# Transposing q and k of the first three units in bf16 to contiguous PSUM columns, with a refitted plan

## The chip, the core and the metric

The kernel runs on one core of a Trainium2 chip. The core's engines work side by side, each through its own queue in order: TensorE (PE in the profile; its weight loads are shown apart as PEld), VectorE (DVE), ScalarE (ACT), GpSimd (POOL) and SyncE (SP), which here mostly issues transfers (DMA). A wait at the head of a queue holds all that stands behind it. The metric is the device time of one execution in microseconds (us). For the kernel before it is 219.11 us, the median of three runs (218.81 to 219.12).

## What is computed

Attention with a local window and a few global keys, followed by a feed-forward block with softplus. The reference, cut to what matters:

```python
# q, k, v: (4, 8, 768, 64), n_global = 8, n_local = 96
scores = np.matmul(q, k.transpose(0, 1, 3, 2)) / np.sqrt(64)
rel = pos[:, None] - pos[None, :]
is_global = pos[None, :] < n_global
is_local = (rel >= 0) & (rel < n_local)
dist = np.where(is_global & ~is_local, n_local, np.abs(rel))
scores = scores - slopes[:, None, None] * dist
a = softmax(np.where(is_global | is_local, scores, -1e9))
x = np.matmul(a, v)                     # then (4 * 768, 8 * 64)
h = x @ w_in                            # w_in: (512, 2048)
g = np.maximum(h, 0.0) + np.log1p(np.exp(-np.abs(h)))
out = g @ w_out                         # w_out: (2048, 512), out: (3072, 512) float32
```

## The kernel before, in words

The 3072 tokens are 24 blocks of 128; two blocks of one batch entry make a unit, and there are 12 units (`UNITS`), numbered in the order in which they are worked on. A unit passes these stages:

- `load_unit` brings q, k and v by DMA into slots `raw`. q and k of the first three units (`WIDE`) come in two halves each, v and everything later in one piece. `load_w` brings slabs of w_in and w_out (`i0` to `i7` and `o0` to `o7`), half a megabyte each. `FIRST_LOADS` lists the first loads, the planner decides their order.
- `cast_q` (L841) and `cast_rows` (L865) convert them to bf16 (`qb`, `kb`, `vb`), on the engine that the table `CHOICE` names. Slabs are converted at L823.
- The transposes bring the head dimension to the partitions (`qT`, `kT`, `kTa`). Units 0 to 2 do this on PE (`transp_pe`, L926), later units by a DMA transpose (`transp_dma`, L953). In `transp_pe` eight matmuls against the identity write f32 to two banks of the scores' PSUM tiles `s_ps`. They write with a step, so that the columns stand in PSUM in the order of `qT`, four apart, and the copy out of PSUM (L936 for one bank of 512 columns, L939 for both banks in one instruction) reads contiguously.
- `scores` (L1058, L1005 for block 0) multiplies, DVE adds the bias into `z` (L1084; blocks 0 and 1 get theirs from PE, L995 and L1039), ACT takes exponentials (L1018, L1091), PE multiplies by v (L1110), DVE divides by the sum (L1121, L1122), PE (L1141) or a DMA transposes the result into `XT`, for the PE ones with a copy at L1146. `globals_k` (L966) and `globals_v` (L976) copy the global keys and values into the block before.
- Two blocks make a group. `mm1` (L1168) multiplies by w_in in eight steps of eight matmuls into two banks `h_ps`; each step is followed by an exponential (L1183), each pair of steps by a logarithm (L1194), which together are the softplus `g`. `mm2` (L1217) multiplies by w_out into `o_ps` (`s_ps` for group 0), `store` copies (L1246) and writes the result (L1249).

The order is not the order of the code. Every piece is an operation of a `Planner`, with an engine, an expected duration and a rank. `due` works ranks back from wanted times and adds a correction of each operation from the table `NUDGE`; `run` then plays the queues and writes the instructions in the order in which they start. Its constants (`FETCH`, `DMA_FIRST` and so on) and its durations shape only that order. Thirty-five dummy matmuls (`filler`, L1330, called `fill0` to `fill34`) have the lowest rank of all: PE gets one whenever nothing else was ready in the plan, until they are used up. The waits in the program follow from what each instruction reads and writes; tiles in PSUM are guarded bank by bank.

Of the kernel before, what the change touches and what calls it, by code (L numbers as in the profile page):

```python
# [23 lines left out]
class Planner:  # L24
# [5 lines left out]
    FETCH = 15.5  # L30
    FETCH_COST = 1.0
    DMA_FIRST = 0.75
# [181 lines left out]
PE_KEYS = {  # L214
# [3 lines left out]
}  # L218
# [47 lines left out]
    "a0.0": -2,  # L266
    "a0.1": -14.5,
    "a0.2": -3,
    "a0.4": 2.25,
    "a1.0": -1,  # L270
    "a1.1": -4.25,
    "a1.2": -3.5,
    "a1.3": -0.5,
    "a1.4": 0.5,
    "a1.6": 15,
    "a1.7": -2,
    "a2.0": 8,
    "a2.2": -11,
    "a2.3": 1.5,
    "a2.4": 4,  # L280
    "a2.5": -10.25,
    "a2.6": -4,
    "a2.7": 8,
    "b0.0.2": 10.5,
    "b0.0.4": -8.5,
    "b0.0.8": -8,
    "b0.1.0": 0.5,
    "b0.1.10": -7.5,
    "b0.1.12": -14.75,
    "b0.1.14": 2.75,  # L290
    "b0.1.2": -1,
    "b0.1.4": 3.75,
    "b0.1.6": -40.75,
    "b0.1.8": 2.75,
    "b1.0.0": 4.75,
    "b1.0.10": 4.5,
    "b1.0.12": -11,
    "b1.0.14": -2,
    "b1.0.2": 1,
    "b1.0.4": -0.5,  # L300
    "b1.0.8": -18.25,
    "b1.1.0": 4.25,
    "b1.1.10": -0.5,
    "b1.1.12": 0.25,
    "b1.1.4": 0.5,
    "b1.1.6": 10,
    "b1.1.8": 55.75,
    "biasFalse0": 2.25,
    "biasFalse2": -2,
    "biasFalse4": 5.5,  # L310
    "biasFalse5": -6.75,
    "biasFalse6": 10,
    "biasFalse7": -5.25,
    "biasTrue0": 1.75,
    "biasTrue2": -2,
    "biasTrue3": 2,
    "biasTrue4": -4,
    "biasTrue6": -0.5,
    "biasTrue7": -1.5,
    "blank": -7,  # L320
    "castk0.0": -2.25,
    "castk0.1": -11.25,
    "castk1.1": 11.5,
    "castk2.0": 4,
    "castk2.1": -8.25,
    "castk3.00": 4.5,
    "castk3.01": -2.5,
    "castk3.10": -0.25,
    "castk3.11": 1,
    "castk4.00": 3.5,  # L330
    "castk4.11": -0.25,
    "castq0.1": 23.25,
    "castq1.1": 16,
    "castq2.0": -17.25,
    "castq2.1": 1.5,
    "castq3.0": 7,
    "castq5.0": 9,
    "castv0.01": 3.5,
    "castv0.10": -1.25,
    "castv0.11": 3,  # L340
    "castv1.00": -13.5,
    "castv1.01": 4,
    "castv1.10": 4,
    "castv1.11": -4.5,
    "castv2.00": 6.5,
    "castv2.01": 8,
    "castv2.10": 8.5,
    "castv2.11": 1.25,
    "castv3.00": 0.75,
    "castv3.10": 0.25,  # L350
    "castv3.11": -20,
    "castv4.00": 1,
    "castv4.10": 0.25,
    "castv4.11": -8,
    "castv6.10": -0.5,
    "castv6.11": -8,
    "cin1": -10,
    "cin2": -3.25,
    "cin3": -67.25,
    "cin4": -0.5,  # L360
    "cin5": -6,
    "cin6": -0.25,
    "cin7": 29,
    "cout0": -6.75,
    "cout1": -19.5,
    "cout3": 0.75,
    "cout4": 2.5,
    "cout6": 6,
    "cout7": -3.25,
    "cpk0.0": -2.75,  # L370
    "cpk1.0": 20.25,
    "cpk1.1": 6.75,
    "cpk2.0": -2,
    "cpk2.1": 9,
    "cpq0.0": 7.25,
    "cpq1.0": -1.25,
    "cpq2.0": 3,
    "d0": -4.25,
    "dl0a": -0.25,
    "dl0b": -0.25,  # L380
    "dl0c": -0.25,
    "dl1a": 0.5,
    "dl1e": 2.5,
    "e0.1": 3.75,
    "e0.2": -4,
    "e0.3": -18.75,
    "e0.4": -1,
    "e0.6": -0.5,
    "e1.0": -2,
    "e1.1": 2,  # L390
    "e1.2": -23,
    "e1.3": 12.5,
    "e1.5": 0.5,
    "e1.6": -1,
    "e1.7": -9.75,
    "e2.3": 2.75,
    "e2.4": -0.5,
    "e2.5": 11.25,
    "ex0.0": 0.75,
    "ex0.1": -8,  # L400
    "ex2.0": -67.75,
    "ex2.1": 2.25,
    "ex3.0": 6.5,
    "ex3.1": -1.5,
    "ex4.0": -23.5,
    "ex4.1": 3.75,
    "ex5.0": -0.25,
    "ex5.1": -26,
    "ex6.0": 0.5,
    "ex6.1": 8.5,  # L410
    "ex7.0": 23.75,
    "ex7.1": 3.75,
    "gk4": 0.5,
    "gk6": 11.75,
    "gk8": 12,
    "gv4.0": -0.75,
    "gv4.1": 1.25,
    "gv5.0": -1,
    "gv5.1": 12,
    "gv6.0": 7,  # L420
    "gv6.1": -6,
    "gv7.1": 0.25,
    "gv8.0": -8,
    "gv8.1": 1,
    "ident": 9.75,
    "iota": -1,
    "ldk0.0": -2,
    "ldk0.1": -6.25,
    "ldk1.0": -5.25,
    "ldk2.0": 0.25,  # L430
    "ldk2.1": 26,
    "ldk3": -4,
    "ldk4": 10.5,
    "ldk5": 1.75,
    "ldq0.0": 1,
    "ldq0.1": 23,
    "ldq1.1": -4,
    "ldq2.0": 12.5,
    "ldq2.1": -4.25,
    "ldq3": -4,  # L440
    "ldv0": 13,
    "ldv3": -8.75,
    "ldv4": -9.5,
    "ldv5": 4,
    "ldv6": -2,
    "ldv7": 16.75,
    "ldv8": 8,
    "ln0.0": 16.5,
    "ln0.2": 4.75,
    "ln0.3": -8.5,  # L450
    "ln1.0": -15,
    "ln1.2": 2,
    "ln2.0": -177.75,
    "ln2.1": 8.75,
    "ln2.2": -8,
    "nm1.0": -12,
    "nm2.0": 7.25,
    "nm2.1": 1,
    "nm3.0": -1,
    "nm3.1": -1,  # L460
    "nm5.0": 2,
    "nm6.0": -12,
    "nm6.1": 1,
    "oc0.0.0": 4,
    "oc0.1.0": 30.25,
    "oc1.0.0": -8,
    "pv0.0": 12,
    "pv0.1": -17.75,
    "pv1.0": -4,
    "pv1.1": 1.25,  # L470
    "pv2.0": 12,
    "pv2.1": -13.75,
    "pv3.0": 0.25,
    "pv3.1": 5.5,
    "pv4.1": 1,
    "pv5.0": -4,
    "pv5.1": 1,
    "pv6.0": 3,
    "pv6.1": -3.25,
    "sb0.0": 2.25,  # L480
    "sb1.1": 17.5,
    "sc0.0": -8,
    "sc1.0": 8,
    "sc1.1": 7.75,
    "sc2.0": 0.5,
    "sc3.0": 9,
    "sc4.0": 7.25,
    "sc5.1": 2,
    "sc6.0": 0.5,
    "sc7.0": -2.25,  # L490
    "st0.0.0": 7.25,
    "st0.1.0": -0.25,
    "st1.0.0": 1,
    "table": -3,
    "trk0.0": 1.5,
    "trk1.0": 1.5,
    "trk1.1": 72.5,
    "trk2.0": -24.5,
    "trk2.1": 1.5,
    "trk4": -2.5,  # L500
    "trq0.0": -36.5,
    "trq1.0": 2,
    "trq2.0": 4,
    "trq2.1": 0.5,
    "trq3": 0.25,
    "trq5": 0.25,
    "win1": -0.5,
    "win5": -16,
    "win6": 1,
    "wout0": -12.5,  # L510
    "wout1": -1.75,
    "wout2": -18.5,
    "wout4": 3.75,
    "wout5": 2,
    "wout7": -11.75,
    "xc1": 5.25,
    "xc2": 1,
    "xc3": 1.75,
    "xc4": 0.25,
    "xc5": -6.5,  # L520
    "xt1": 2,
    "xt2": -82.5,
    "xt4": 5.25,
    "xt5": -2,
    "xt6": -6.75,
    "z2.0": 0.25,
    "z3.0": -8.25,
    "z4.0": -2,
    "z4.1": 15,
    "z5.0": -2,  # L530
    "z6.0": 8,
    "z6.1": -47.25,
# [22 lines left out]
    "biasFalse0": "POOL",  # L555
    "biasFalse2": "DVE",
    "biasFalse5": "DVE",
    "biasTrue0": "DVE",
    "biasTrue1": "DVE",
    "biasTrue2": "DVE",  # L560
    "biasTrue3": "POOL",
# [5 lines left out]
    "castk2.0": "POOL",  # L567
    "castk3.00": "ACT",
    "castk3.01": "ACT",
    "castk3.10": "DVE",  # L570
    "castk3.11": "ACT",
    "castk4.00": "DVE",
    "castk4.01": "ACT",
    "castq0.0": "POOL",
# [3 lines left out]
    "castq4.0": "POOL",  # L578
    "castq5.0": "POOL",
    "castv0.00": "DVE",  # L580
    "castv0.01": "POOL",
    "castv0.10": "ACT",
    "castv1.00": "DVE",
    "castv1.01": "POOL",
    "castv1.10": "DVE",
    "castv2.11": "ACT",
    "castv3.00": "ACT",
    "castv3.01": "DVE",
    "castv3.10": "ACT",
    "castv3.11": "DVE",  # L590
    "castv4.01": "ACT",
    "castv4.10": "ACT",
    "castv4.11": "ACT",
    "cin1": "ACT",
    "cin3": "DVE",
    "cin5": "DVE",
    "cin6": "DVE",
    "cout3": "ACT",
    "cout6": "DVE",
    "cout7": "DVE",  # L600
    "cpk0.0": "DVE",
    "cpk1.1": "ACT",
    "cpk2.1": "DVE",
    "cpq0.0": "ACT",
    "cpq2.1": "ACT",
    "gk4": "ACT",
    "gk5": "ACT",
    "gk6": "ACT",
    "gk7": "ACT",
    "gv4.0": "ACT",  # L610
    "gv4.1": "ACT",
    "gv5.0": "ACT",
    "gv6.0": "DVE",
    "gv8.0": "DVE",
    "oc0.0.0": "ACT",
    "xc1": "ACT",
    "xc4": "ACT",
# [13 lines left out]
def kernel(  # L631
# [116 lines left out]
    def held(keys):  # L748

        return sorted({key[:2] for key in keys})  # L750
# [13 lines left out]
    def load_unit(i, rank, only="qkv"):  # L764
# [4 lines left out]
        for z, which in enumerate(only):  # L769
# [25 lines left out]
            op(f"ld{which}{i}", "SP", 0.45, rank + 0.01 * z, fn, dma=(2.5 if (which, i) == ("v", 0) else 1.8, 30.0), sync=sync,  # L795
# [95 lines left out]

    def kt_unit(i):
        name, slot = kt_tile(i)
        return {"kTa": kTa, "kT": kT}[name][slot][:]
# [16 lines left out]
    def v_keys(n):  # L911
        return [("vb", vb_slot(n), r) for r in range(2)]

    def transp_pe(i, which, banks, engs, rank):


        src = {"q": qb, "k": kb}[which][i % NQB][:].rearrange("p a h d -> p (a h d)")
        dst = qT[i % NQT][:] if which == "q" else kt_unit(i).rearrange("p x m t -> p (x m) t")
        for rs in ((0, 1),) if len(held(banks)) == 1 else ((0,), (1,)):

            def mm(rs=rs):
                for r in rs:
                    tr = bank(banks[r]).rearrange("p (x m g a) -> p a x g m", x=2, m=NPAIR, a=4)
                    for a in range(4):
                        c = P * (2 * a + r)
                        nc.tensor.matmul(tr[:, a], src[:, c : c + P], ident[:])  # L926
# [573 lines left out]
```

## Time and profile before

| what | us |
|---|---|
| median of the runs | 219.11 |
| the profiled execution's own time | 219.03 |
| its span in the trace | 217.2 |
| PE busy | 211.7 |
| ACT busy | 170.7 |
| DVE busy | 115.7 |
| POOL busy | 74.4 |
| transposes of q and k on PE: from 6.79 to 33 us, 48 matmuls | 5 of the chain of waits |

The page gives, for each engine, busy time and share of the span, and then the span in 40 slices of 5.43 us, each with a digit for the busy share (9 is 90% or more). The chain of waits is followed back from the last instruction: at each step to whatever released it. The timeline lists instructions in order of start: start in us, duration, engine, line, operation, tile written `<-` tiles read, shape, count; in square brackets stands the engine's idle time before it and who ended it. The duration of a matmul includes the time to pass through the array, and consecutive matmuls overlap, so their pace is read from start to start. The granted TensorE clock is full in every slice.

### The profile page before, as it was taken

How to read it: one execution, taken by the hardware profiler on the slowest of the kernel's cores; microseconds unless marked ns; L12 is line 12 of the kernel's file. 1: busy time of each engine (PE TensorE's matmuls, PEld its weight loads, DVE VectorE, ACT ScalarE, POOL GpSimd, SP SyncE). 2: the span in 40 equal slices, each digit the busy share in tenths (PEclk: the TensorE clock that was granted, in tenths of full speed). 3: DMA queues.
4: the chain of work that ended last, by engine and by line, in shares of the span. 5: the costliest groups of instructions: out<-in, count | busy, mean ns of one | idle time of the engine just before them, and what ended most of it. 6: DMA issues, size and time to landing. Idle time of an engine off the chain costs nothing.

```text
span 217.2 us, 4970 instructions
## 1 busy us (share of the span) xinstructions
PE 211.7 (97%) x2003; PEld 144.5 (67%) x2003; DVE 115.7 (53%) x216; ACT 170.7 (79%) x236; POOL 74.4 (34%) x127
## 2 busy tenths in 40 slices
PE   7899999999999999999999999999999999999994
PEld 2576887656665787757767767756766767767554
DVE  6568868674489667327546546446545952101121
ACT  4899999999995699978788688678697878788300
POOL 6316333253059525900265274233236320000000
PEclk9999999999999999999999999999999999999999
DMA  5999999999999399945895996892687212011112
GB/s 202 333 367 387 386 357 367 317 286 214 225 317 175 104 236 264 211 108 155 147 231 160 159 218 165 207 165 72 127 209 198 69 30 75 0 48 53 48 48 97
DMA packets 69846, 40.95 MB, mean 188 GB/s; under 512 B 30144, under 2 KB 61248, under 8 KB 69824
## 3 DMA queue, kind: packets, MB, share of 16 engines
q1 hardware_dynamic: 69392, 40.05, 72.1%
q10 hardware_dynamic: 432, 0.59, 0.9%
q8 instruction: 15, 0.25, 0.5%
q14 instruction: 7, 0.06, 0.1%
HBM read 27.26 MB, written 6.29 MB: 154 GB/s over the span
## 4 chain that ended last, share of the span: by engine, by line
PE 83%; ACT 12%; DMA 2%; issue 2%; SPq 0%; DVE 0%
PE h_ps L1168 34%; PE o_ps L1217 30%; PE s_ps L1058 5%; PE x_ps L1110 4%; ACT pb L1091 3%; ACT e L1183 3%; PE s_ps L1217 3%; PE s_ps L926 2%; DMA raw<-in_k_dram 2%; PE x_ps L1217 2%; ACT g L1194 2%; PE x_ps L1330 1%; ACT vb L976 1%; ACT XT L1146 1%; ACT kb L865 1%
## 5 line engine op out<-in xcount | busy, mean ns | idle before, releaser
L1168 PE MATMUL h_ps<-XT,w_in_bf 128*128 128x256 bf16 x768 | 95.8, 273 | 0.9 <-ACT e L1183 0.7
L1168 PEld LDWEIGHTS <-w_in_bf 128*128 128x128 bf16 x768 | 73.6, 98 | 18.7 <-issue 1.7
L1217 PE MATMUL o_ps<-w_out_bf,g 128*128 128x512 bf16 (+1 forms) x320 | 77.7, 371 | 0.0
L1183 ACT ACTIVATE e<-h_ps 128x512 f32<-128x512 f32 x96 | 59.5, 627 | 20.9 <-PE h_ps L1168 20.5
L1217 PEld LDWEIGHTS <-g 128*128 128x128 bf16 x416 | 37.3, 98 | 28.6
L1084 DVE TENSOR_TENSOR z<-s_ps,biasA 128x1024 f32<-128x1024 f32 x38 | 45.8, 1219 | 15.2 <-PE s_ps L1058 8.6
L1194 ACT ACTIVATE g<-e 128x1024 bf16<-128x1024 f32 x48 | 50.7, 1057 | 1.3
L1091 ACT ACTIVATE pb<-z 128x1024 bf16<-128x1024 f32 (+1 forms) x44 | 43.1, 988 | 7.9 <-DVE z L1084 7.9
L1246 DVE COPY osb<-o_ps 128x512 f32<-128x512 f32 (+1 forms) x20 | 13.4, 670 | 37.1 <-PE o_ps L1217 37.1
L976 POOL COPY vb<-vb 4x512 bf16<-4x512 bf16 x27 | 16.4, 608 | 33.0 <-PE x_ps L1110 28.6
L865 POOL CAST vb<-raw 64x512 bf16<-64x512 f32 x33 | 20.4, 617 | 18.0 <-DMA raw<-in_v_dram 16.8
L865 POOL CAST kb<-raw 64x512 bf16<-64x512 f32 x30 | 18.6, 619 | 19.5 <-DMA raw<-in_k_dram 18.4
L1110 PEld LDWEIGHTS <-pb 128*128 128x128 bf16 x352 | 16.5, 98 | 6.1 <-ACT pb L1091 0.2
L1122 DVE TENSOR_TENSOR xs<-x_ps,rcp 128x256 bf16<-128x256 f32 x40 | 17.0, 424 | 1.4
L1121 DVE RECIPROCAL rcp<-x_ps 128x4 f32<-128x4 f32 x40 | 7.2, 179 | 18.7 <-PE x_ps L1110 18.3
L1110 PE MATMUL x_ps<-vb,pb 128*128 128x65 bf16 x304 | 15.9, 193 | 0.0
L1217 PE MATMUL s_ps<-w_out_bf,g 128*128 128x512 bf16 (+1 forms) x64 | 13.6, 352 | 0.0
L1330 PE MATMUL x_ps<-blank 128*128 128x512 bf16 x35 | 11.1, 442 | 1.2 <-DVE blank L1269 1.2
L1058 PEld LDWEIGHTS <-kT 64*128 64x128 bf16 x224 | 6.8, 94 | 5.1 <-issue 4.9
L1058 PE MATMUL s_ps<-qT,kT 64*128 64x128 bf16 x224 | 9.9, 218 | 0.0
L1084 DVE TENSOR_TENSOR z<-s_ps,bias 128x512 f32<-128x512 f32 x6 | 3.9, 687 | 7.3 <-PE s_ps L1058 7.3
L1246 ACT COPY osb<-x_ps 128x128 f32<-128x128 f32 x1 | 0.3, 266 | 8.7 <-PE x_ps L1217 8.7
(84 smaller groups left out, 120.7 us busy)
## 6 DMA issues: line engine op xcount, KB each, us to landing
raw<-in_v_dram SPq DMA_DIRECT2D x12, 512.0 KB, 5.7
out_dram<-osb SPq DMA_DIRECT2D x23, 256.0 KB, 2.3
raw<-in_q_dram SPq DMA_DIRECT2D x9, 512.0 KB, 4.5
raw<-in_k_dram SPq DMA_DIRECT2D x9, 512.0 KB, 5.6
raw<-in_moe_w_in_dram SPq DMA_DIRECT2D x8, 512.0 KB, 9.5
raw<-in_moe_w_out_dram SPq DMA_DIRECT2D x8, 512.0 KB, 8.6
raw<-in_k_dram SPq DMA_DIRECT2D x6, 256.0 KB, 6.0
raw<-in_q_dram SPq DMA_DIRECT2D x4, 256.0 KB, 8.0
```

Source lines behind the costliest of these rows:

```text
L865: copy_on[eng](dst, src)
L976: copy_on[eng](vb_of(prev)[sl, :, 0:D], vb_of(first)[sl, :, 0:D])
L1058: nc.tensor.matmul(reg if unit_of(n) in WIDE else reg.rearrange("p (r t) -> p r t", r=2), kt[rows, 2 * part + m, :], qv(rows, 2 * part + m ...
L1084: nc.vector.tensor_tensor(z, src, bias, ALU.add)
L1091: nc.scalar.activation(pb[:, 0:nr, :].rearrange("p (y a) b -> p y (a b)", y=2), src, AF.Exp, scale=1.0 / root_d)
L1110: nc.tensor.matmul(xv[:, h, :], pb[:, 4 * (h % 2) + 2 * part + h // 2 if lone else u_all * (2 * (h % 2) + h // 2) + u, :], vb_of(prev if u ...
L1122: nc.vector.tensor_tensor(xs[:, 4 * part : 4 * part + 4, :], xv[:, :, 0:D], rcp[:][:, :, None].to_broadcast([P, 4, D]), ALU.mult,)
L1168: last = nc.tensor.matmul(hv[:, j, :], w_in_bf[:, m, fb * P : fb * P + P], XT[g % NXG][:, m, :], start=(m == 0), stop=(m == NM - 1),)
L1183: nc.scalar.activation(e[:, p % 2, :, :].rearrange("p j (b t r) -> p (j b) r t", b=2, r=2), hb[:].rearrange("p (a r t) -> p a r t", a=4, r=2),
L1194: nc.scalar.activation(gt[:, 2 * p - 2 : 2 * p + 2, :].rearrange("p a t -> p (a t)"), e[:].rearrange("p a j t -> p (a j t)"), AF.Ln, bias=1.0,
L1217: nc.tensor.matmul(bank(key)[:, 0 : z - a], gt[:, fb, ns * P : ns * P + P], w_out_bf[:, fb, a:z], start=(fb == 0), stop=(fb == NFB - 1),)
L1246: copy_on[eng](osb[:, a:z], bank(key)[:, 0 : z - a])
```

## The change

Four things change, of which the last reorders the whole program:

- In `transp_pe` the eight transposes of one matrix write bf16 into one PSUM bank, each to 128 contiguous columns, rather than f32 with a step into two banks. The step moves into the copies: each half (512 columns) is read with four nested steps, the innermost over `a`, 128 columns apart, and written contiguously.
- There are always two copies of 512 for one matrix, each on an engine of its own by `CHOICE` (DVE or ACT); both read the same bank. Before, units 0 and 1 had three copies of 1024 and two of 512, unit 2 had four of 512.
- `globals_k` spells its access with one dimension more, for the same elements.
- The planner's constants, the tables `NUDGE` (every correction) and `CHOICE` (casts, biases and copies put on other engines) are fitted anew. So the order on every queue differs, that of the first loads on SP too. `FIRST_LOADS`, the sizes of the loads and the number of dummies stay.

```diff
-    FETCH = 15.5
+    FETCH = 18.0
-    DMA_FIRST = 0.75
+    DMA_FIRST = 0.62
...
 PE_KEYS = {
-    0: (("s", 1, 0), ("s", 1, 1), ("s", 0, 0), ("s", 0, 1)),
-    1: (("s", 1, 0), ("s", 1, 1), ("s", 0, 0), ("s", 1, 0)),
-    2: (("s", 0, 0), ("s", 1, 0), ("s", 1, 0), ("s", 0, 0)),
+    0: (("s", 0, 0), ("s", 1, 0)),
+    1: (("s", 1, 0), ("s", 0, 0)),
+    2: (("s", 0, 0), ("s", 1, 0)),
 }
...
-    def transp_pe(i, which, banks, engs, rank):
+    def transp_pe(i, which, key, engs, rank):
         src = {"q": qb, "k": kb}[which][i % NQB][:].rearrange("p a h d -> p (a h d)")
...
-            def mm(rs=rs):
-                for r in rs:
-                    tr = bank(banks[r]).rearrange("p (x m g a) -> p a x g m", x=2, m=NPAIR, a=4)
-                    for a in range(4):
-                        c = P * (2 * a + r)
-                        nc.tensor.matmul(tr[:, a], src[:, c : c + P], ident[:])
...
-            def ev(eng, rs=rs):
-                if len(rs) == 1:
-                    to = dst[:, :, 64 * rs[0] : 64 * rs[0] + 64]
-                    copy_on[eng](to, bank(banks[rs[0]]).rearrange("p (c t) -> p c t", t=64))
-                else:
-                    to = dst.rearrange("p c (r t) -> p r c t", r=2)
-                    copy_on[eng](to, s_ps[banks[0][1]][:].rearrange("p r (c t) -> p r c t", t=64))
...
+        tr = bank(key).bitcast(BF16)
+
+        def mm():
+            for r in range(2):
+                for a in range(4):
+                    c, z = P * (2 * a + r), P * (4 * r + a)
+                    nc.tensor.transpose(tr[:, z : z + P], src[:, c : c + P], ident[:])
...
+        for r in range(2):
+
+            def ev(eng, r=r):
+                copy_on[eng](
+                    dst[:, :, 64 * r : 64 * r + 64].rearrange("p (x m) (g a) -> p x m g a", x=2, a=4),
+                    tr[:, 512 * r : 512 * r + 512].rearrange("p (a x g m) -> p x m g a", a=4, x=2, g=16),
+                )
...
-    op("table", "ACT", 1.3, TABLE_RANK, table, writes=["table"])
+    op("table", "ACT", 0.1, TABLE_RANK, table, writes=["table"])
```

What this makes of the order in the built program, as far as the prediction needs it. The first transposes are q0's and then k0's (before: k0's, q0's). Dummies stand in runs of 14, 7, 5, 5, 2 and 2, the last of them before the transposed results of block 1; before, the last one stood right ahead of the first `mm1`. SP issues after k0 and the first half of q1: v0, q1, slab i0, k1, i1, i3, k1, i2, v1, i4 and so on; before it was v0, q1, q1, k1, i3, k1, v1, i1, i0, i2, i4.

More of the change, by code (lines that the diff above doesn't have):

```diff
@@ new lines @@
+    "biasFalse6": 2.25,
+    "biasTrue0": -2,
+    "biasTrue1": 18.5,
+    "biasTrue3": -5,
+    "biasTrue4": 10.75,
+    "biasTrue7": 0.25,
+    "blank": -7.5,
+    "castk1.1": 3.5,
+    "castk2.0": -7.25,
+    "castk3.00": -0.5,
+    "castk3.01": 1.5,
+    "castk3.10": -2.5,
+    "castk4.00": -7,
+    "castk4.01": -2.5,
+    "castk4.10": 6,
+    "castk4.11": -6.5,
+    "castk5.00": 4,
+    "castq0.0": 0.25,
+    "castq0.1": -2,
+    "castq1.0": -2.25,
+    "castq1.1": -32,
+    "castq2.0": 5.75,
@@ new lines @@
+    "cpq1.0": 0.25,
+    "cpq1.1": -1.5,
+    "cpq2.0": 1.25,
+    "d0": -10.75,
+    "d0e": -4.75,
+    "dl0a": 14,
+    "dl0b": 21.5,
+    "dl1c": -5.5,
+    "e0.0": 2,
+    "e0.1": -21.75,
+    "e0.2": 1,
+    "e0.3": -32.75,
+    "e0.5": -35.25,
+    "e0.6": -8.25,
+    "e0.7": -1.25,
+    "e1.0": 8.75,
+    "e1.1": -38.25,
+    "e1.2": 8,
+    "e1.5": -1,
+    "e1.7": 0.5,
+    "e2.2": -10.75,
+    "e2.3": 2,
+    "e2.5": 3.25,
+    "e2.7": 10,
+    "ex0.0": -7.25,
+    "ex0.1": -17.25,
+    "ex1.0": 8,
@@ new lines @@
+    "ex1.1": -2,
+    "ex2.0": -11.25,
+    "ex2.1": 4,
+    "ex3.0": 1.5,
+    "ex3.1": 1,
+    "ex4.0": 4,
+    "ex4.1": -2,
+    "ex5.1": -5.25,
+    "ex6.0": -1.25,
+    "ex6.1": 2,
+    "ex7.0": -8.75,
+    "ex7.1": 16.5,
+    "gk4": 1,
+    "gk5": 9.25,
+    "gk6": 0.25,
+    "gk7": 5,
+    "gk8": -2.75,
+    "gv4.0": -8.25,
+    "gv5.0": -8.25,
+    "gv6.0": -1,
+    "gv6.1": 14,
+    "gv7.1": 0.25,
+    "gv8.0": -4,
+    "gv8.1": 8,
+    "ident": -0.25,
+    "iota": 9.75,
+    "ldk0.1": -2.75,
@@ new lines @@
+    "win0": -24.5,
+    "win1": 4.5,
+    "win2": 1.5,
+    "win3": -17.5,
+    "win4": -2.5,
+    "win5": -4.5,
+    "win6": 0.5,
+    "win7": -4,
+    "wout0": 3,
+    "wout1": -0.75,
+    "wout2": 5,
+    "wout3": -1,
+    "wout5": 3,
+    "wout6": -0.25,
+    "wout7": 1.25,
+    "xc1": -0.5,
+    "xc3": -17.75,
+    "xc4": -12.75,
+    "xt1": -6.5,
+    "xt2": -9.25,
+    "xt3": -23.25,
+    "xt4": -4.5,
+    "xt5": -20.25,
+    "xt6": -6.75,
+    "z2.0": -31.75,
+    "z2.1": -7,
+    "z3.0": 3,
@@ L533 @@
+    "z3.1": 1.75,
+    "z4.0": 8,
+    "z4.1": 1,
+    "z5.0": 0.5,
+    "z5.1": -23.25,
+    "z6.0": 13.25,
+    "z6.1": -1,
     "z7.0": 0.5,
@@ L567 @@
     "castk2.0": "POOL",
+    "castk2.1": "DVE",
     "castk3.00": "ACT",
-    "castk3.01": "ACT",
-    "castk3.10": "DVE",
-    "castk3.11": "ACT",
     "castk4.00": "DVE",
-    "castk4.01": "ACT",
-    "castq0.0": "POOL",
+    "castk4.10": "DVE",
+    "castk4.11": "ACT",
     "castq0.1": "ACT",
@@ new lines, in transp_pe @@
+        dst = qT[i % NQT][:] if which == "q" else kT_t(i)[:].rearrange("p x m t -> p (x m) t")
+        tr = bank(key).bitcast(BF16)
[4 more added lines that the diff above has]
+                    nc.tensor.transpose(tr[:, z : z + P], src[:, c : c + P], ident[:])
+        op(f"tr{which}{i}.0", "PE", 0.45, rank, mm, count=8,
+           reads=[(which + "b", i % NQB, x) for x in range(4)] + ["ident"], writes=held([key]))
@@ new lines, in transp_pe @@
+        for r in range(2):
[4 more added lines that the diff above has]
+                )
+            outs = [("qT", i % NQT, r)] if which == "q" else [kt_tile(i) + (x, r) for x in range(2)]
+            op(f"cp{which}{i}.{r}", engs[r % len(engs)], 0.0, rank + 0.1 * r, ev, reads=held([key]), writes=outs,
+               alts={e: t_copy(e, 512) - (0.07 if e == "DVE" else 0.0) for e in ("DVE", "ACT")})
```

509 lines of the change are left out of this document (201 added, 308 removed).

## The prediction

> **What bounds the kernel now.** I read the busy shares first, then the 40 slices, then the chain of waits, then the timelines of TensorE (PE) and ScalarE (ACT) over the first 62 us.
>
> ```profile
> PE 211.7 (97%) x2003; PEld 144.5 (67%) x2003; DVE 115.7 (53%) x216; ACT 170.7 (79%) x236; POOL 74.4 (34%) x127
> ...
> PE   7899999999999999999999999999999999999994
> ...
> ACT  4899999999995699978788688678697878788300
> ```
>
> PE has hardly an idle tenth after the second slice, so the time is PE's work, plus its dummy matmuls (35 of them, L1330), plus 5.5 us idle (217.2 less 211.7), of which 1.17 stands at the start and some 2.8 behind the last matmul. ACT is as full up to 65 us. The chain of waits, cut to its first 62 us, says who leads there:
>
> ```profile
> 6.79 1.92 PE s_ps L926 x16
> ...
> 17.07 1.04 ACT w_in_bf L823
> ...
> 27.49 1.91 PE h_ps L1168 x16
> ...
> 47.99 0.58 ACT g L1194
> ...
> 49.47 1.91 PE h_ps L1168 x16
> ```
>
> Up to 16 us the chain runs through PE and the transposes (L926); from 16.5 to 49.4 us mostly through ACT, with PE full beside it; from 49.5 us to the end through PE alone. So work taken from PE pays only if ACT's queue in the first 49 us gets shorter too.
>
> **Transposes.** PE's timeline:
>
> ```profile
> 6.79 1.05 PE L926 MATMUL s_ps<-ident,kb 128*128 128x128 bf16 x8 [0.62 <-ACT kb L841]
> 7.63 1.08 PE L926 MATMUL s_ps<-ident,qb 128*128 128x128 bf16 x8
> 8.51 0.64 PE L995 MATMUL h_ps<-bias,ident 128*128 128x256 bf16 x4
> ...
> 17.53 0.40 PE L1141 MATMUL o_ps<-ident,xs 128*128 128x128 bf16 x4
> 17.76 1.03 PE L1330 MATMUL x_ps<-blank 128*128 128x512 bf16 x4
> ```
>
> Starts are what counts: 16 scattered f32 transposes take from 6.79 to 8.51, 107 ns each. The kernel already has transposes in bf16 to contiguous PSUM columns: four at L1141 take from 17.53 to 17.76, 57 ns each. All 48 L926 transposes become that kind: 48 x 50 ns = **2.4 us less PE work**. The 16 of unit 2 (29 to 33 us) lie where PE is full: 0.8 us. The other 32 lie among dummies, where only an earlier arrival of data pays. Dummies stay 35, so they hide nothing on balance.
>
> **Copies.** Rows:
>
> ```profile
> 7.88 1.23 DVE L939 CAST kTa<-s_ps 128x1024 bf16<-128x1024 f32 x1 [2.38 <-PE s_ps L926]
> 8.75 1.01 ACT L939 CAST qT<-s_ps 128x1024 bf16<-128x1024 f32 x1
> ...
> 30.31 0.69 DVE L936 CAST qT<-s_ps 128x512 bf16<-128x512 f32 x1 [0.95 <-PE s_ps L926]
> ```
>
> Six copies of 512 and three of 1024 become twelve of 512, reading bf16 with a step of 128 elements. No row has that read. ACT bounds: 0.57 (contiguous bf16, L1146, and f32, L936) and, if every element cost double, 1.0; I take 0.57. DVE bounds: 0.42 (contiguous bf16, L1146 at 23.75) and 1.2 (double the f32 one); I take 0.69, the f32 row, since a wide step gives no reason to expect the fast one. [...]
>
> Both halves now lie in one PSUM bank. In the built program the second engine's copy waits for the first engine's (ACT for DVE at q0 and k2, DVE for ACT at k0 and k1). So a pair split over two engines takes 0.65 + 0.1 + 0.55, some 1.3 us, no less than the one 1024 copy of before (1.01 or 1.23). [...]
>
> **The front, step by step.** Order from the built program, durations from the rows. ACT casts k0's first half at 4.70, then q0's first half (0.6), two biases (0.5), q0's second half, k0's second half: 7.1 for q0, 7.7 for k0. Transposes: q0 7.1 to 7.6, k0 7.75 to 8.2. DVE copies q0's first half to 8.3, ACT its second to 8.95 and k0's first to 9.5, DVE k0's second to 10.2. First scores at 10.25; they stood at 10.16 before. **No gain there**: the serial copies eat it. ACT then casts v0 twice and q1 once, so the first exponentials start at 11.4 instead of 10.95. PE gets to q1's transposes at 13.45 (13.22 before), and has 5 + 2 dummies before k1's, which can start at 16.3; k1's second load half now stands behind two w_in slabs and lands near 15.5 (4.0 MB, against 4.5 MB at the 16.9 at which POOL's wait for a slab ends in this trace). k1's transposes end 16.75, ACT's copy 17.55, DVE's 18.25, scores of unit 1 18.3 to 18.6. XT of group 0 is whole by 18.1 to 18.65, so w_in's first group starts at 18.65, against
>
> ```profile
> 20.06 1.91 PE L1168 MATMUL h_ps<-XT,w_in_bf 128*128 128x256 bf16 x16
> ...
> 22.45 1.03 PE L1168 MATMUL h_ps<-XT,w_in_bf 128*128 128x256 bf16 x8 [0.36 <-ACT e L1183]
> ```
>
> The second slab cast that this needs moved on ACT from 17.07 to about 13.5, since its load goes out earlier; that, fewer dummies ahead (all 35 end before 17.3 instead of at 20), and shorter transposes are where the front gains. v1 pays for it: its load stands behind three slabs (5.0 MB instead of 3.5) and lands near 18.1 instead of
>
> ```profile
> 14.21 0.61 POOL L865 CAST vb<-raw 64x512 bf16<-64x512 f32 x1 [3.57 <-DMA raw<-in_v_dram]
> ```
>
> On ACT two casts of v1 stand ahead of the exponentials of block 2 and of the first softplus exponentials, on DVE one ahead of block 2's bias addition: DVE 18.1, 19.0, 19.65; ACT ends exp of block 2 at 20.2, softplus exp 20.75. PE's third w_in group starts at 20.9: 1.55 earlier than 22.45. PE has by then left out 4 value matmuls (0.13) and 8 scores (0.33) that stood ahead of it: 1.1 us net.
>
> **Does ACT follow?** To its second softplus exponential it gets at 21.85 instead of 22.9: 1.05 ahead. From there to the last logarithm of group 1, the order has 1.0 us less on ACT: three k casts, one v cast, one XT copy and one copy of the global keys less (1.86 + 0.62 + 0.47 + 0.11), one exponential, one q cast and one XT copy more (0.94 + 0.62 + 0.47). POOL takes the casts (34% busy). So ACT is 2.05 ahead at 46 us, PE 1.1 + 0.8 = 1.9. PE stays the limit.
>
> **Sum.** 1.1 + 0.8 less 0.3 for new gaps (before has 0.36 and 0.35 of such, on softplus exponentials): 1.6 us. Slab loads keep 1.2 to 1.6 us of margin by the same megabytes, so they hide. Behind 49 us the instructions are the same, reordered; distances between producer and consumer in PE work stay above the latencies of the rows in both orders, so nothing there. The profiled execution took 219.03 (span 217.2 and 1.83 around it), 0.08 below the median of 219.11. 219.03 - 1.6 gives **217.4 us**, span 215.6.
>
> **Rivals.**
> - *The front gains nothing (0.20).* Strided reads cost double, or k1's chain of load, cast, transposes and two serial copies holds unit 1 until 20 us. For it: that chain has no slack. Left: 0.8 for unit 2 less 0.3: 218.5.
> - *Everything pays (0.17).* DVE's copies take 0.42 and v1 lands a us earlier, so that the front gains 2.2 net and no gaps come: 219.03 - 3.0 gives 216.0. Against it: ACT must follow, and is only 2.05 ahead.
> - *Slower: v1's load (0.18).* ACT and DVE stand in order behind v1's casts; each us that v1 lands later moves the softplus exponentials, hence the third w_in group. It decides at 1.9 us of delay, a landing past 20.0. ACT would be late by as much and, being the limit to 49 us, never make it up; a landing at 21.3 gives 1.3 - 0.3 and with gaps behind it about 220.1. For it: DMA is full from 5 to 45 us (shares above 1.0 in the stages), and POOL waited 3.57 for v1 already. Against it: 5.0 MB at the rate of this trace.
> - *It doesn't do what it says*: the built program has 48 transposes to 128 contiguous columns, so no chance of its own.
>
> **Chances.** Forecast 0.45 (own range 216.8 to 218.2), rivals as given. About 0.2%, 0.44 us, is what a measurement can tell from no change. Half of the first rival falls within that: faster 0.45 + 0.17 + 0.10 = 0.72, same 0.10, slower 0.18. The range from 216.0 to 219.6 takes in the DVE bounds and the first half of the slow case.
>
> **What would show it.** Transposes at 57 ns from start to start; if 107, bf16 brought nothing. A DVE copy of 0.69, ACT's 0.57, never overlapping in one bank. First scores at 10.2, first w_in group at 18.7, third at 20.9, v1's cast at 18.1. Group 2's first w_in matmuls at 47.6 instead of 49.47, and the rest moved by the same. Wrong if ACT idles over 1 us for v1, or if PE, without dummies, idles more than a us between 20 and 50.

## The result, and the profile after

The changed kernel takes **218.33 us** (median of 22 runs, 217.66 to 219.66), against 219.03 for the kernel before on the same chip (22 runs, 218.34 to 220.13): a ratio of 0.9975, 95% interval 0.9964 to 0.9986. It is faster, by 0.7 us where 1.6 were forecast. The profiled execution took the median, 218.33; its span is 216.6 (217.2 before).

The page of the changed kernel, the rows that were shown of before:

```profile
PE 208.8 (96%) x1974; PEld 142.4 (66%) x2003; DVE 116.0 (54%) x220; ACT 166.6 (77%) x227; POOL 78.8 (36%) x135
...
PE   7897999999999999999999999999999999999994
...
ACT  4798999996895699978788688678697878778300
```

PE is still the full engine. Its 208.8 must not be set against the 211.7 of before: 29 of the 2003 matmul records are missing here (x1974). Marks in the timeline serve better. PE's timeline of the changed kernel, front (start, duration, line, operation; idle time before it in brackets):

```profile
7.51 0.61 PE L938 MATMUL s_ps<-ident,qb 128*128 128x128 bf16 x8
7.96 0.61 PE L938 MATMUL s_ps<-ident,kb 128*128 128x128 bf16 x8
8.41 1.67 PE L1335 MATMUL x_ps<-blank 128*128 128x512 bf16 x7
...
18.83 0.40 PE L1063 MATMUL s_ps<-qT,kTa 64*128 64x128 bf16 x8 [0.75 <-DVE kTa L945]
...
22.04 1.05 PE L1173 MATMUL h_ps<-XT,w_in_bf 128*128 128x256 bf16 x8
```

The 16 transposes go from 7.51 to 8.41, 56 ns each, where before had 107. But the third w_in group, forecast for 20.9, starts at 22.04, only 0.41 before the 22.45 of the old kernel, and 0.46 of that is work (four value matmuls, eight scores) which the new order does later. So the front has gained nothing in this execution. Who holds it is told by DVE's and ACT's timelines:

```profile
9.99 0.69 DVE L945 COPY kTa<-s_ps 128x512 bf16<-128x512 bf16 x1 [1.14 <-ACT kTa L945]
...
18.08 0.69 DVE L945 COPY kTa<-s_ps 128x512 bf16<-128x512 bf16 x1 [0.48 <-ACT kTa L945]
18.69 0.41 DVE L1151 COPY XT<-h_ps 128x512 bf16<-128x512 bf16 x1
19.13 0.84 DVE L875 CAST vb<-raw 64x512 bf16<-64x512 f32 x1
20.00 1.29 DVE L1089 TENSOR_TENSOR z<-s_ps,bias 128x512 f32<-128x512 f32 x2
```

```profile
18.98 1.25 ACT L875 CAST vb<-raw 64x512 bf16<-64x512 f32 x2 [0.27 <-DMA raw<-in_v_dram]
20.79 0.63 ACT L1096 ACTIVATE pb<-z 128x512 bf16<-128x512 f32 x1 [0.56 <-DVE z L1089]
```

ACT casts v1 at 18.98, as soon as it has landed, rather than at 18.1. But ACT is through with both casts at 20.23 and then waits 0.56 for DVE, so in this execution v1's landing is not what holds the front. DVE is busy until 19.10 with k1's second copy, which waited for ACT's, and with a copy to `XT`. Its own cast of v1 then takes 0.84 instead of 0.42 (before's, at 16.88, took 0.43), so the bias addition of block 2 starts at 20.00, ACT's exponential of it at 20.79 (PE's value matmuls wait 0.39 for it), and the first softplus exponential at 21.32. The chain of waits, cut to the first 62 us, runs through the same places (start, us, what):

```profile
6.91 8.91 DMA raw<-in_k_dram
...
15.84 0.67 DVE kb L851
...
17.46 0.59 ACT kTa L945
...
18.08 0.69 DVE kTa L945
18.77 0.33 DVE XT L1151
...
19.13 0.84 DVE vb L875
...
20.00 0.70 DVE z L1089
```

So here it is the second half of k1: its load ends at 15.81 (forecast near 15.5), and its two copies, one behind the other, end at 18.77 (forecast 18.25). v1 came close behind; the experiments will show it as the last in other executions.

From there the chain of before led through ACT to 49 us; here PE takes over at 27.56. Between 23 and 50 us PE shows no wait of 0.2 us or more. Block 9's scores, the next mark used below, start at 67.98 (68.56 before), group 3's first w_in at 72.52 (73.10): 0.58 ahead, and that stays to the end.

### The profile page after: what moved, and what is told of

It reads as the page before. It is cut to its first block, busy times and chain, and to the rows that moved or that the text cites. A ratio compares the mean times of both kernels' runs of the same rounds, so it can differ in the third digit from the quotient of the medians.

```text
span 216.6 us, 4949 instructions
## 1 busy us (share of the span) xinstructions
PE 208.8 (96%) x1974; PEld 142.4 (66%) x2003; DVE 116.0 (54%) x220; ACT 166.6 (77%) x227; POOL 78.8 (36%) x135
## 4 chain that ended last, share of the span: by engine, by line
PE 86%; DMA 6%; ACT 3%; DVE 2%; issue 1%; SPq 1%; ACTq 0%
PE h_ps L1173 37%; PE o_ps L1222 30%; PE s_ps L1222 6%; PE s_ps L1063 5%; PE x_ps L1115 5%; DMA raw<-in_k_dram 4%; DMA raw<-in_q_dram 2%; PE x_ps L1222 2%; ACT pb L1096 1%; ACT e L1188 1%; SPq L790 1%; PE s_ps L938 1%; ACT g L1199 0%; DVE vb L875 0%; DVE z L1089 0%
## 5 line engine op out<-in xcount | busy, mean ns | idle before, releaser
L1222 PE MATMUL o_ps<-w_out_bf,g 128*128 128x512 bf16 (+1 forms) x295 | 73.6, 371 | 1.2
L875 POOL CAST vb<-raw 64x512 bf16<-64x512 f32 x38 | 23.3, 614 | 15.7 <-DMA raw<-in_v_dram 14.4
L875 POOL CAST kb<-raw 64x512 bf16<-64x512 f32 x32 | 19.6, 613 | 22.8 <-DMA raw<-in_k_dram 21.6
L1222 PE MATMUL s_ps<-w_out_bf,g 128*128 128x512 bf16 (+1 forms) x62 | 13.0, 352 | 0.1
L1335 PEld LDWEIGHTS <-blank 128*128 128x128 bf16 x35 | 3.7, 117 | 5.9 <-issue 3.3
```

The costliest lines, as they stand in the source:

```text
L875: copy_on[eng](dst, src)
L1222: nc.tensor.matmul(bank(key)[:, 0 : z - a], gt[:, fb, ns * P : ns * P + P], w_out_bf[:, fb, a:z], start=(fb == 0), stop=(fb == NFB - 1),)
L1335: nc.tensor.matmul(x_ps[:], blank[:, 0:P], blank[:])
```

## The experiments

Fifteen kernels were run, each against the kernel before on the same chip (its medians there: 218.97 to 219.13). The marks are from one profiled execution of each; the medians are of 6 to 22 runs. Executions of one program differ by up to a microsecond in the front (e10 below), so the column of the third group says less than the distance "9 - 3rd" from it to block 9's scores, or the medians. In e1 and e3 two of the 16 scores of block 9 start earlier (67.31 and 66.80); the table has the other 14. e6 to e8 failed and stand further down.

| kernel | v1's casts on ACT at | third w_in group | block 9's scores | 9 - 3rd | median us | ratio to before, 95% |
|---|---|---|---|---|---|---|
| before | 15.33 | 22.45 | 68.56 | 46.11 | 219.03 | |
| after | 18.98 | 22.04 | 67.98 | 45.94 | 218.33 | 0.9975 [0.9964, 0.9986] |
| e4 old plan | 14.80 | 21.93 | 67.94 | 46.01 | 218.32 | 0.9963 [0.9946, 0.9981] |
| e5 old transposes | 19.45 | 22.35 | 68.91 | 46.56 | 220.02 | 1.0053 [1.0024, 1.0082] |
| e1 two tiles | 18.94 | 21.37 | 67.95 | 46.58 | 218.28 | 0.9954 [0.9936, 0.9972] |
| e2 loads | 18.96 | 22.46 | 68.41 | 45.95 | 218.65 | 0.9979 [0.9965, 0.9993] |
| e3 both | 18.49 | 20.89 | 67.97 | 47.08 | 218.22 | 0.9965 [0.9948, 0.9982] |
| e10 after, copy moved | 18.51 | 21.09 | 67.00 | 45.91 | 218.00 | 0.9952 [0.9931, 0.9973] |
| e12 tiles, copy moved | 19.61 | 22.04 | 67.99 | 45.95 | 218.13 | 0.9950 [0.9922, 0.9979] |
| e13 loads, copy moved | 18.81 | 22.05 | 67.97 | 45.92 | 218.48 | 0.9968 [0.9952, 0.9984] |
| e9 both, copy moved | 18.72 | 21.11 | 66.98 | 45.87 | 217.27 | 0.9916 [0.9885, 0.9948] |
| e11 as e9, fewer dummies | 18.78 | 22.23 | 68.11 | 45.88 | 217.59 | 0.9944 [0.9910, 0.9979] |
| e15 as e9, XT first | 18.43 | 20.83 | 66.74 | 45.91 | 217.95 | 0.9939 [0.9921, 0.9957] |
| e14 v1 later | 21.48 | 23.97 | 70.26 | 46.29 | 220.17 | 1.0042 [1.0020, 1.0064] |

**Theories.** A: the front loses its gain in the serial copies of one matrix. B: it loses it to v1's load. C: whatever the front gains is cut further behind. D: the refitted order, not the transposes, carries the gain.

### One part alone: e4 and e5

e4 is before's plan with bf16 transposes to contiguous columns and stepped copies:

```diff
-                    tr = bank(banks[r]).rearrange("p (x m g a) -> p a x g m", x=2, m=NPAIR, a=4)
+                    tr = bank(banks[r]).bitcast(BF16)
...
-                        nc.tensor.matmul(tr[:, a], src[:, c : c + P], ident[:])
+                        nc.tensor.transpose(tr[:, P * a : P * a + P], src[:, c : c + P], ident[:])
```

> The kernel before, plan and order untouched, with only the transposes changed: bf16 to contiguous columns, in the banks that the old plan gave them, and copies that read with four steps (where it had one copy of 1024, two of 512 on the same engine). If the transposes alone carry the result and the refit nothing: 0.5 to 1.0 us under the kernel before (unit 2's 0.8 us, less two small copies), 218.0 to 218.5, like the changed kernel. If the refit carries it: within 0.2 us of the kernel before. If the front of the old plan, whose first 20 us on PE have no gap, turns all 2.4 us into time: 216.6 to 217.2.

218.32: as much as the whole change. e5 is the opposite, after's plan with f32 transposes with a step, in two banks of one tile:

```diff
-        tr = bank(key).bitcast(BF16)
+        tr = [bank(("s", key[1], r)) for r in range(2)]
...
-                    nc.tensor.transpose(tr[:, z : z + P], src[:, c : c + P], ident[:])
+                    nc.tensor.matmul(to[:, a], src[:, c : c + P], ident[:])
```

> After's plan and order, but the 48 transposes write f32 with a step again, to the two banks of one PSUM tile, and the copies read contiguously, twelve of 512. Computes the same. It isolates the refitted plan: what of the change's 0.7 us comes from the order alone. Theory: all of it comes from the cheaper transposes (the old plan with new transposes alone took 218.32, as much as after), so this kernel loses PE's 16 x 50 ns of unit 2 and, since the first two units' chain is late already, part of the 32 x 50 ns before: 218.9 to 219.8, no better than before. Rival, the new order is worth something by itself: 218.3 to 218.6, little above after. Copies at 0.69 on DVE and 0.57 on ACT under both.

220.02, just above the theory's range, and slower than before. So theory D falls: the order alone brings no gain. By the medians the transposes are worth 0.7 in the old order and 1.7 in the new one, and the new order costs 1.0 with the old transposes and nothing with the new. The 1.7 and the 1.0 are loose: e5's runs fall into two groups, seven at 219.0 to 220.1 and five at 221.2 to 221.7, and its trace is from the lower one; why is open. The marks say where. e4 has its third group 0.52 earlier than before, in the same order, but to block 9's scores it takes 46.01 against 46.11: of unit 2's 0.8 only 0.1 arrives, in part since PE waits there for ACT and DVE (0.27, 0.25 and 0.22 us; before had 0.35). After takes 45.94 against e5's 46.56, again in one order: 0.62 arrives. By these marks the old order pays in the front and loses unit 2's part, the new one the other way round.

e5 also tells what makes the copies of one matrix wait for each other. Its halves lie in two banks of one tile, and its copies are serial all the same (DVE's second copy of kTa waits 1.14 for ACT's first, as in after); with two tiles (e1, next) they overlap (DVE's copy of qT runs from 7.68 to 8.37, ACT's starts at 7.91). So for these copies the program guards a PSUM tile as a whole, and not bank by bank as the description of the kernel has it.

### The front: e1, e2 and e3

e1 puts the halves of q0, k0 and k1 into two PSUM tiles; the order stays:

```diff
-        tr = bank(key).bitcast(BF16)
+        split = {
+            ("q", 0): (("s", 0, 0), ("s", 1, 0)),
+            ("k", 0): (("s", 1, 1), ("s", 0, 1)),
+            ("k", 1): (("s", 1, 0), ("s", 0, 0)),
+        }.get((which, i))
+        if split:
+            tr = [bank(split[r]).bitcast(BF16)[:, 0:512] for r in range(2)]
```

> The changed kernel in its own order, but the halves of q and k of unit 0 and of k of unit 1 go to two PSUM tiles instead of one, so that ACT's and DVE's copies no longer wait for each other. Theory A (the serial copies ate the gain of the front): first scores at 9.7 instead of 10.74 us, ACT's queue starts its copies 0.6 to 0.7 earlier, the first w_in group moves by 0.5 or more, and the time falls by 0.4 to 0.8 us against the changed kernel, to 217.5 to 217.9. Theory B (the late loads of k1's second half and of v1 hold the front): first scores earlier, but k1's cast still waits for its load until 15.8 and DVE's cast of v1 until 19.0; first w_in group moves by less than 0.6 us, the second softplus exponential not at all, the time by less than 0.2: 218.2 to 218.4.

e2 issues two loads earlier on SP:

```diff
+    order.remove(at["ldk1.1"])
+    order.insert(order.index(at["win3"]), at["ldk1.1"])
+    order.remove(at["ldv1"])
+    order.insert(order.index(at["win3"]), at["ldv1"])
```

> The changed kernel with its order on all engines but SP, where the loads of k1's second half and of v1 go ahead of the w_in slabs i3 and i2. Theory B: k1's second half lands near 14.3, v1 near 16.5 instead of 19.0, the waits of ACT and DVE for them go, block 2's bias addition starts 0.5 us or more earlier, and the time falls by 0.4 to 0.7 us against the changed kernel: 217.6 to 217.9. Theory A: the loads are hidden behind the chain of the copies, ACT has no gap there to close, less than 0.2: 218.2 to 218.4. If the slabs i3 and i2 now come too late for the third w_in group, POOL waits for them and the time rises.

e3 has both edits.

> Both edits together. If A and B name two links of one chain, each alone gains little and both together 0.8 to 1.2 us: 217.1 to 217.5, close to what was forecast for the change. If the front's gain is lost behind it (ACT is full from 20 to 47 us and cannot follow), the third w_in group starts up to 1 us earlier but the end moves by less than 0.3: 218.0 to 218.4.

e1's copies overlap, its first scores start at 9.31 (10.74 in after) and the third group at 21.37. e2 by itself gains nothing: 22.46. e3's third group starts at 20.89, **where the forecast had it, at 20.9**. And yet all three take 218.2 to 218.7: e1 lies in the range of theory B though its front moved as A had it, e2 is above both of its ranges, and e3 lies where the gain is lost behind the front. The table shows the place: e1 and e3 begin the bulk of block 9's scores at 67.95 and 67.97, after at 67.98, though their fronts were 0.67 and 1.15 ahead. PE's timeline of e3 there:

```profile
66.80 0.23 PE L1071 MATMUL s_ps<-qT,kT 64*128 64x128 bf16 x2
67.97 0.56 PE L1071 MATMUL s_ps<-qT,kT 64*128 64x128 bf16 x14 [0.94 <-POOL kT L979]
```

and POOL's queue in e3:

```profile
64.46 2.58 POOL L875 CAST kb<-raw 64x512 bf16<-64x512 f32 x4 [1.69 <-DMA raw<-in_k_dram]
67.15 0.61 POOL L875 CAST vb<-raw 64x512 bf16<-64x512 f32 x1
67.71 0.20 POOL L979 COPY kT<-kTa 128x32 bf16<-128x32 bf16 x1
```

PE starts two of the 16 scores, then waits 0.94 for the small copy of the global keys into block 9, which stands in POOL's queue behind five casts of unit 5, and these wait for a load. In e1 it is the same (a wait of 0.41), and in both the chain of waits that ended last runs through this queue. The copy ends at 67.55 in before, 67.33 in after, 67.89 in e1, 67.91 in e3: a wall near one moment. After reaches block 9 0.65 behind its copy, so that the wall costs its profiled execution nothing; but the better fronts of e1 and e3 meet a load that lands later (their casts start behind it at 64.60 and 64.46, after's at 64.03 without a wait for it), and only some 0.1 us of them gets past. Theory C, then.

### A failed edit: e6, e7 and e8

The five casts were moved behind the copy:

```diff
+    for n in ["castv5.00", "castk5.00", "castk5.11", "castk5.10", "castk5.01"]:
+        order.remove(at[n])
+        order.insert(order.index(at["gk9"]) + 1, at[n])
```

> The kernel with two PSUM tiles and the earlier loads of k1 and v1 (both edits of the front), with one more: on POOL, the five casts of unit 5's k and v that stand ahead of the copy of the global keys into block 9 (L979) move right behind it. Computes the same. In the kernel without this edit PE waits 0.94 us at 67.97 for that copy, which ends 67.9 because the casts ahead of it wait for the load of unit 5's k (landed 64.4). Theory: POOL's queue at this place is the wall at which the front's gain is lost; then the wait of 0.94 goes, PE's work at 70 us is 0.9 ahead of where it was, and the time is 217.1 to 217.5. Rival: the load itself, or the transposes by DMA behind it, are the limit, and the scores of unit 5 wait instead some us later: 218.0 to 218.4, with a new wait of PE of about 0.9 between 68 and 80 us.

> The changed kernel with the same move on POOL alone: the five casts of unit 5 behind the copy of the global keys into block 9. Computes the same. Theory: in the changed kernel PE reaches block 9's scores 0.5 us after that copy, so that the wall does not bind there, its own loss lying in the front; then nothing changes, 218.1 to 218.5. Rival: POOL's queue costs the changed kernel its missing microsecond too: 217.2 to 217.6.

> The kernel with both edits of the front and the move on POOL, without the last four of the 14 dummy matmuls that stand ahead of the first transposes (31 dummies are left; they only write an unused tile). Computes the same. In the changed kernel's profile these 14 run from 1.17 to 7.1 us at 0.43 us each, and end 0.3 to 0.5 us after the casts that the transposes need. Theory: they hold the front, so the first transposes start about 0.4 us earlier and the time falls by 0.1 to 0.4 against the kernel with the same edits and all dummies. Rival: casts and loads hold the front, or with fewer dummies PE comes to its full pace later and the transposes run at half pace: no change within 0.2, or slower by 0.1 to 0.5.

226.14, 225.85 and 226.04 us: 7 us more, foreseen by no theory. Between the casts and the copy SP's DMA transpose of unit 5's keys stood in the order. Moved past it, the casts had to wait for it (POOL of e7 waits 7.10 us for it), and the transpose took the keys of unit 3 for those of unit 5. These three say nothing of the wall. What had to move was the copy.

### The wall taken away: e9, e10, e11 and e12

The copy goes ahead of the casts; it needs nothing that comes later. e9 does it to e3, e10 to after, e12 to e1; e11 is e9 without the dummies `fill10` to `fill13`.

```diff
+    order.remove(at["gk9"])
+    order.insert(order.index(at["castk5.01"]), at["gk9"])
```

> The kernel with two PSUM tiles and the earlier loads of k1 and v1, and on POOL the copy of the global keys into block 9 (L979) ahead of the first cast of unit 5's k, rather than behind five casts of unit 5. Nothing else is moved, and it computes the same. (The earlier attempt moved the casts instead, and so also past the DMA transpose of unit 5's keys, which then took the keys of unit 3 and made the casts wait for it: it says nothing of the wall.) Theory: POOL's queue at this place is the wall at which the front's gain is lost; the copy can start by 64.1, the wait of 0.94 at 67.97 goes, and the time is 217.1 to 217.5. Rival: a later wait takes its place (the DMA transposes of unit 5, or ACT), PE has lost the same 0.9 by 80 us: 218.0 to 218.4.

> The changed kernel with this one move on POOL: the copy of the global keys into block 9 ahead of unit 5's casts. Computes the same. Theory: the changed kernel reaches block 9's scores 0.5 us after that copy, so the wall does not bind, and its loss lies in the front: 218.1 to 218.5. Rival: POOL's queue costs the changed kernel its missing microsecond: 217.2 to 217.6.

> The kernel with two PSUM tiles alone (loads as in the changed kernel), with the global keys' copy ahead of unit 5's casts. Computes the same. It shows what the serial copies by themselves cost once the wall is gone, against the changed kernel with the same move. Theory: with two tiles PE's work stood 0.7 to 0.8 us ahead of the changed kernel's at 60 us, of which 0.1 was left behind the wall; now all stays: 217.4 to 217.8. Rival: another wait takes it: 218.1 to 218.4, as without the move.

> The kernel with both edits of the front and the global keys' copy moved, without the last four of the 14 dummy matmuls ahead of the first transposes (31 dummies are left; they only write an unused tile). Theory: the dummies, at 0.43 us each until PE doubles its pace, end 0.3 to 0.5 us after the casts that the transposes need, so that without four of them the transposes start about 0.4 earlier: 0.1 to 0.4 less than the kernel with all dummies. Rival: casts and loads hold the front, or PE comes to its full pace later: no change within 0.2, or 0.1 to 0.5 more.

e9: 217.27, in the theory's range, 0.95 less than e3 (the intervals of their ratios just meet, at 0.9948). **Theory C holds**: block 9's scores start at 66.98 without a wait, and "9 - 3rd" is 45.87 to 45.95 in every kernel with the copy moved and in after, but 46.58 in e1 and 47.08 in e3. Some of it is lost a little further on; PE's timeline of e9:

```profile
72.14 1.92 PE L1181 MATMUL h_ps<-XT,w_in_bf 128*128 128x256 bf16 x16 [0.45 <-DMA XT<-xs]
```

e10: 218.00, a little under the theory's range, far from the rival's. Its profiled execution explains the little: with the same instructions as after up to 60 us it had v1 at 18.51, its third group at 21.09 and a span of 215.7. So executions of one program differ by a microsecond in the front, and the wall may cut the quick ones; by the medians this is not shown, since the intervals of e10 and after overlap. e12: 218.13, a miss; two tiles no longer help where v1 lands at 19.61, as in its profile (third group 22.04). e11: 217.59, no gain over e9; in its profile PE waits 1.54 for ACT's cast of q0, so that there casts and loads hold the first transposes, as the rival had it.

### Loads alone, and v1 later: e13, e14 and e15

e13 is e2 with the copy moved.

> The changed kernel with the earlier loads of k1 and v1 (ahead of slabs i3 and i2) and the global keys' copy ahead of unit 5's casts; halves still in one PSUM tile. Computes the same. With the kernels that have neither, tiles only, and both of the front's edits, all with the copy moved (218.0, 218.1, 217.3), it fills the square. Theory: with the wall gone, what the front loses in most executions is v1's landing (between 18.5 and 19.6 in the profiles so far, forecast 18.1), and two tiles help only once v1 is there: 217.3 to 217.8. Rival: the serial copies of k1 hold unit 1 as well, so that loads alone bring nothing: 217.9 to 218.3.

218.48: a miss, a little above the rival's range too, and the rival's case by its trace. Its unit-1 scores wait 0.75 for DVE's second copy of kTa and start at 18.91; DVE's cast of v1 stands behind that copy, at 19.21, although v1 is there. So with the wall away, neither tiles (218.13) nor loads (218.48) gain against e10's 218.00, and both together do (217.27), though the intervals of e9 and e10 overlap, and e11 and e15, which have both edits too, stand at 217.59 and 217.95.

The chains of waits say it more plainly than the medians. In after, e2 and e13 the chain enters DVE's cast of v1 from k1's two serial copies. In e10, e1 and e12 it comes from v1's load and goes through ACT's casts; in e10:

```profile
8.64 9.85 DMA raw<-in_v_dram
...
18.51 0.62 ACT vb L875
...
19.14 0.62 ACT vb L875
...
19.84 0.63 ACT pb L1096
```

In e3 and e9 it does neither, and runs to a later slab of w_in; e11's and e15's, with both edits too, reach the casts of v1 through other work. After and e10 have the same instructions in the front, and one shows each case: the two waits end within 0.5 us of each other (ACT is through with v1 at 20.23 and the bias addition at 20.70 in after, at 19.76 and 19.75 in e10). So **A and B hold together**, each hiding behind the other.

e14 moves v1's load behind one more slab:

```diff
+    order.remove(at["ldv1"])
+    order.insert(order.index(at["win4"]) + 1, at["ldv1"])
```

> The changed kernel with v1's load moved one place back on SP, behind slab i4 (half a megabyte). Computes the same. It doubles the suspected wait. Theory: v1 lands 1.2 to 1.4 later (19.8 to 21), ACT and DVE stand behind its casts, the third group of w_in starts 0.7 to 1.4 after the 22.04 of the changed kernel, and the time is 218.8 to 219.7. Rival: casts and copies, not v1, set the front: third group within 0.3 of 22.04, 218.1 to 218.6.

v1 is cast at 21.48, 2.5 later than in after and above the theory's range, and so is the time: 220.17, 1.84 more. PE's timeline of e14:

```profile
23.41 0.30 PE L1115 MATMUL o_ps<-vb,pb 128*128 128x65 bf16 x4 [2.58 <-ACT pb L1096]
```

The wait of 2.58 is for the exponential that stands behind v1's casts on ACT. In this order most of a later landing of v1 goes into the time.

e15 is e9 with SP's DMA transpose of unit 5's keys behind that of block 7's result.

```diff
+    order.remove(at["trk5"])
+    order.insert(order.index(at["xt7"]) + 1, at["trk5"])
```

> The kernel with two PSUM tiles, earlier loads and the copy moved, with SP's DMA transpose of block 7's result issued ahead of the one of unit 5's keys, which waits for POOL's casts. Computes the same. In the kernel without this edit PE waits 0.45 at 72.14 for a transposed result. Theory: SP's queue is the next wall behind POOL's; the wait goes: 216.7 to 217.2, PE's work at 80 us no more than 0.2 behind that at 70. Rival: the transposes themselves or another wait (scores of block 10, whose keys now come later) take its place: 217.2 to 217.6.

The wait at 72 us is gone and group 3's first w_in starts at 71.28, but the median is 217.95, outside both ranges and above e9's 217.27, with overlapping intervals. Whether the edit brings anything stays open. The intervals of e9 and e15 both lie below the changed kernel's; e9, the best, is 0.8% (0.5 to 1.2) faster than before, by six runs.

## Why the prediction was off, point by point

- **Transposes**: right. 56 ns for 57; unit 2's 0.8 arrives as 0.62 (after against e5).
- **Copies**: right. DVE 0.69, ACT 0.59 where 0.69 and 0.57 were taken; the four steps cost nothing above the f32 row (0.69 on DVE and 0.58 to 0.59 on ACT in before). That the two halves wait for each other was right too; but they do so in two banks of one tile as well (e5), so it is the tile that the program guards. Two tiles are worth 0.65 us at the first scores (e1's stand 1.43 ahead of after's, of which an earlier start of the transposes makes 0.78), but in the end nothing while v1 is late.
- **The front, step by step: the step that failed.** 1.1 net was forecast, and -0.05 came (22.45 to 22.04, less 0.46). The path was right: k1's second copy on DVE, DVE's cast of v1 and bias addition, ACT's exponentials. Its terms were mis-sized. *k1 "lands near 15.5", its second copy ends at 18.25*: 15.81 and 18.77, 0.52 late. *DVE's cast of v1*, 0.42 by the forecast's own times: 0.84, beside POOL's, another 0.42. The last 0.2 lies in the bias addition and the exponentials. These make up the 1.14 between 20.9 and 22.04. *"v1 lands near 18.1"* was too early as well, by 0.4 to 1.5: it is there at 18.5 to 19.6 in the executions that wait for it with this order of loads (after, e1, e5, e10, e12). In after it is just in time to cost nothing more; in e10's execution of the same instructions it is the last. *First transposes at 7.1*: 7.51, since the 14 dummies ahead of them took until 7.1 where before's pace had been assumed; that delays the first scores (10.74 for 10.25), but in after the chain goes by k1's load instead; in e13, where that load comes earlier, it goes through these dummies. In an execution in which nearly all went well (e10's) k1's second copy ends at 18.23 and the third group is at 21.09, 0.9 net: the sum described the best case, not the usual one. That this execution took 217.46, next to the forecast's 217.4, is chance.
- **Does ACT follow**: right. PE waits no more between 23 and 50 us; without the refit it does (e4).
- **"Behind 49 us ... nothing there": failed as well**, though the changed kernel doesn't show it. The distance between producer and consumer was looked at for the old lead of PE, not for one of 1.9. e3 met the forecast's front and took 218.22, not 217.4: POOL's wall takes nearly all of it. Only with the copy moved, and both edits of the front, does the time come near the forecast's (e9, 217.27). The mark for group 2's first w_in matmuls, 47.6, failed even with the front as forecast: 49.75 in after, 48.56 in e3.
- **New gaps, 0.3**: none of 0.2 or more between 23 and 50. By these marks what came is unit 2's 0.62 less the front's 0.05, and the spans differ by 0.6.
- **Rivals**: the time is near that of "the front gains nothing" (218.5), not by its strided reads but by its other branch, k1's chain of load and serial copies, whose lack of slack it names (it puts unit 1 at 20 us; it was 18.83). v1's load, put down as the slower case with a threshold of 20.0, is the other wait, and it costs before that threshold too (e12's lands at 19.6, 1.1 after e10's, and its third group starts 0.95 later). Its price, 220.1 for a landing at 21.3, is close to e14's median of 220.17; the cast at 21.48 is from an execution that took 220.85. "Everything pays" (216.0) came in no run; e9 is the nearest, at 217.27.
- **Signs of being wrong**: neither showed. ACT waited 0.27 for v1, not over 1 us, and PE shows one wait of 0.39 between 20 and 50. The signs looked behind the place where the gain was lost: PE's longer waits, 0.66 and 0.75, stand ahead of 20 us.

What stays open: why loads and PE's pace differ by up to a microsecond between executions of one program.

## What to carry to other kernels

When a change shortens an early stage, follow its lead through every engine's queue to the end and ask of each small operation that PE waits for what stands ahead of it: here a 0.2 us copy behind five casts that wait for a load let only some 0.1 of 1.15 us through. Take a refitted plan apart from the edit it serves, and price each load that it moves back by the order in which engines stand behind its casts. If two waits end close to each other, undoing one shows nothing; undo both, and then each alone, and read in the chain of waits which of them ended last.

## What the runs showed of the hardware

- PE's pace at the start. The 14 dummies from 1.17 on take 4.5 to 6.2 us in 13 profiled executions (6.07 in after, 5.15 in e10 with the same instructions). They go at 0.43 each until the pace doubles: their weight loads start 0.43 apart up to 4.56 in before and up to 6.69 in after, and seven more dummies, at 8.41 in after, take 1.67. In e11, with ten dummies ahead, the four bias matmuls at 5.41 still take 1.06, where after's at 7.08 take 0.60. The granted clock is put at 0.998 to 1.000 for these executions. What sets the moment of the doubling is not shown.
- DVE and POOL casting at once. DVE's cast of 64x512 f32 takes 0.42 when it starts 0.10 or 0.02 ahead of POOL's cast (e1 and e10, where POOL's then takes 0.80 and 0.88) and 0.84 when it starts 0.06 behind it (after, where POOL's takes 0.62). Started 0.06 behind POOL's copy of 0.61, which POOL's cast of a slab follows, it took 1.81 (e11). No run moves POOL's cast of v1 alone, so the cause is not shown.
